# Attention and expert routing on one core: the value products of a tile shared by two heads, written alternately

## The chip, the cores and the metric

One core of a Trainium2 chip runs the whole program in one launch. The metric is device time in microseconds (us). The five engines are TensorE (PE, with its weight loads as PEld), VectorE (DVE), ScalarE (ACT), GpSimd (POOL) and SyncE (SP, which issues most DMAs).

## The reference

Eight batches of eight heads attend over 576 positions of 64 numbers. Each row of scores keeps its 32 largest, and the softmax of those weighs the values. The result, 4608 rows of 512, goes through a layer of eight experts.

```python
scores = scale * np.matmul(q, k.transpose(0, 1, 3, 2))
kth = np.partition(scores, -top_k, axis=-1)[..., -top_k:-top_k + 1]
scores = np.where(scores >= kth, scores, -1000000000.0)
attn = np.exp(scores - np.max(scores, axis=-1, keepdims=True))
attn = attn / (np.sum(attn, axis=-1, keepdims=True) + 1e-09)
return np.matmul(attn, v).astype(np.float32)
```

## The kernel before, in words

The attention (`attention`) works on 32 pairs of heads. The 576 rows of a head are four tiles of 128 and one of 64, so a pair has nine tiles: tiles 0 to 3 are the first head's, 5 to 8 the second's, and tile 4 is shared, with the last 64 rows of the first head on partitions 0 to 63 and those of the second on 64 to 127.

For each tile, `tile_ops` (L203) sets down a chain over four engines. PE computes the scores into the PSUM tile `s` (L216, one of three buffers). DVE finds the 24 largest by six partial maxima (L219) and five steps on their results (L222 to L226). ACT takes a sign (L231). PE moves the ones found out of the way (L234 with `off`), DVE finds the next eight (L237, L238), PE moves them back (L234 with `back`), and ACT writes a mask `r` (L241), which frees `s`. `soft` (L268) then computes the scores again, transposed and masked, in PSUM (L279, L284, L285). ACT takes the exponential into `F`, or into `E` for tile 4 (L289), and POOL splits `F` into two 16-bit parts `ehm` and `elm` (L292, L295). `tail` does the same for the last 64 keys, in `E4`, and in `E4r` for tile 4.

`values` (L346) multiplies the exponentials by the values. For each of the eight tiles of one head alone, `dot` sets down part 0, twelve 16-bit matmuls over four blocks of keys, and part 1, one 32-bit matmul with `E4`. Tile 4 isn't split: each of its two heads has four 32-bit matmuls with `E` as part 0 and one with `E4r` as part 1. Their weights are 64 columns wide, and the heads write to partitions 0 to 63 and 64 to 127 of one PSUM tile. All of these are L363. Then DVE adds a constant to the sums and inverts them (L343, L377), and ACT scales the rows (L345).

```python
p=None; cnt=0
for j in range(2 if g==1 else 4):
    need=[P["vready"]]+([P["ev"][4],P["e4ready"]] if g==1 else [P["ev"][j if g==0 else 5+j],P["e4op"]])
    sp=(4 if g==1 else j if g==0 else 5+j) in SPLIT
    for part in range(2):
        p=at(t0+O["vd"]*cnt,lambda j=j,part=part,dot=dot: dot(j,part),[p]+need,take="pt" if j==0 and part==0 else None,e="P",d=.224 if part else .36 if sp else .9); cnt+=1
```

The order in which each engine's instructions stand is not that of the loops. `at` hands each step to a planner (`Plan`) with a priority (a due time `t` from the table `O`), what it must follow, the engine, and a cost `d` in microseconds. `run` plays the steps through by these costs and emits each engine's instructions in the order that results. On the chip every engine then runs its instructions in that order. So a cost given to a step changes the order of all engines, while the step takes what it takes.

After attention, `logits` (L396 to L420) multiplies the rows by the gate, and the expert layer (`moe`) follows with a planner of its own.

Of the kernel before, what the change touches and what calls it, by code (L numbers as in the profile page):

```python
# [20 lines left out]
class Plan:  # L21
# [10 lines left out]
    def at(self, t, f, pre=(), take=None, free=(), e=None, d=0.0, late=0.0, order=()):  # L32

        pre, order = ([p for p in l or () if p is not None] for l in (pre, order))
        op = dict(t=t, f=f, n=len(pre) + len(order), next=[], pre=pre, order=order, take=take, left=0, free=[], e=e, d=d, late=late)
        for p in pre + order: p["next"].append(op)
        for taker in free or (): self.frees(op, taker)
        self.ops.append(op)
        return op
# [60 lines left out]
def attention(tc, q,k,v,w_gate,x_out,L,acc,cuts, pairs):  # L100
# [3 lines left out]
    with ExitStack() as ctx:  # L104
# [6 lines left out]
        V,G,A,T=nc.vector,nc.gpsimd,nc.scalar,nc.tensor  # L111
# [32 lines left out]
        at=loom.at  # L144
# [196 lines left out]
        def norm(av,n_,dst):  # L341
            r=wk.tile([128,4,1],F32,tag="rs",name="rs",bufs=4)
            V.tensor_scalar(r[:,:n_],av[:,:,64:65],VS*1e-9,None,op0=ALU.add)  # L343
            return r
        def scale(av,r,j,dst): A.activation(dst[:,j,:],av[:,j,0:64],AF.Copy,scale=r[:,j,:])  # L345
        def values(P):  # L346

            n=P["n"]; hp=P["hp"]; last=[]
            for g in (0,1,2):
                t0=(n*9+8)*PER+O["v%d"%g]  # L350
                D={}; n_=1 if g==1 else 4
                def begin(D=D,n_=n_):
                    pv=ps_t.tile([128,512],F32,tag="pt",name="pv"); D["av"]=pv[:,:n_*65].rearrange("p (j d) -> p j d",d=65)
                def dot(j,part,D=D,g=g,begin=begin):
                    if j==0 and part==0: begin()
                    av=D["av"]; vt,vh,vl=P["vt"],P["vh"],P["vl"]
                    h=0 if g==0 else 1
                    if g!=1: e_=P["e"][j if h==0 else 5+j]; out=av[:,j,:]; cs=lambda c: slice(c*128,c*128+128); last=P["e4"][:,j*128:j*128+128]
                    else: h=j; e_=P["e"][4]; out=av[h*64:h*64+64,0,:]; cs=lambda c: slice(c*128+h*64,c*128+h*64+64); last=P["e4r"]
                    if type(e_) is tuple: seq=[(e_[x][:,cs(c)],v_[:,h,c,:]) for c in range(4) for (x,v_) in ((0,vh),(0,vl),(1,vh))]  # L360
                    else: seq=[(e_[:,cs(c)],vt[:,h*5+c,:]) for c in range(4)]
                    seq.append((last,vt[:,h*5+4,:])); N=len(seq)
                    for m_ in (range(N-1) if part==0 else (N-1,)): T.matmul(out,seq[m_][0],seq[m_][1],start=(m_==0),stop=(m_==N-1))  # L363
                def dst(g=g):
                    xb,xr=P["x"]
                    return xr[:,hp:hp+1,:] if g==1 else xb[:,:,(2*hp+(0 if g==0 else 1))*64:(2*hp+(0 if g==0 else 1))*64+64]
                p=None; cnt=0
                for j in range(2 if g==1 else 4):
                    need=[P["vready"]]+([P["ev"][4],P["e4ready"]] if g==1 else [P["ev"][j if g==0 else 5+j],P["e4op"]])
                    sp=(4 if g==1 else j if g==0 else 5+j) in SPLIT  # L370
                    for part in range(2):
                        p=at(t0+O["vd"]*cnt,lambda j=j,part=part,dot=dot: dot(j,part),[p]+need,take="pt" if j==0 and part==0 else None,e="P",d=.224 if part else .36 if sp else .9); cnt+=1
                        if j==0 and part==0: tp=p
                for i in ((0,1,2,3),(4,),(5,6,7,8))[g]: loom.frees(p,P["teh"][i])
                loom.frees(p,P["te4r" if g==1 else "te4"])
                def sums(D=D,n_=n_): D["r"]=norm(D["av"],n_,None)
                def inv(D=D,n_=n_): V.reciprocal(D["r"][:,:n_],D["r"][:,:n_])  # L377
                p=at(t0+O["vd"]*cnt+O["vn"],sums,[p],e="V",d=.07); p=at(t0+O["vd"]*cnt+O["vn"]+.05,inv,[p],e="V",d=.09)
                for j in range(n_): p=at(t0+O["vd"]*cnt+O["vs"],lambda D=D,j=j,dst=dst: scale(D["av"],D["r"],j,dst()),[p],free=[tp] if j==n_-1 else None,e="A",d=.198)
                last.append(p)  # L380
            P["done"]=at(p["t"]+.001,lambda: None,last+[P["clear"]])
# [41 lines left out]
        for n in range(len(pairs)):  # L423
            prep(n); P=Ps[n]; b=P["b"]
            P.update(st=None,tr={},mx={},rel={},q2={},ev={},teh={},soft={},x=[None,None])
            first=P["hp"]==0
            def begin(P=P,n=n,first=first):
                P["st"]=wk.tile([128,9,33],F32,tag="st",name="st",bufs=3)
                P["x"]=(wk.tile([128,4,512],F32,tag="xb",name="xb",bufs=2),wk.tile([128,4,64],F32,tag="xr",name="xr",bufs=2)) if first else Ps[n-1]["x"]
            pre=[Ps[n-3]["done"]] if n>2 else []  # L430
            if n: pre.append(Ps[n-1]["begin"])
            if first and b>1: pre.append(batch[b-2])
            P["begin"]=at(n*9*PER+O["S"]-0.01,begin,pre)
            for i in range(9): tile_ops(P,i)
            for i in range(9): soft(P,i)
            clear(P)
            tail(P)
            values(P)
            if P["hp"]==2: logits(P,0)
            if P["hp"]==3:  # L440
                P["done"]=at(P["done"]["t"]+.001,lambda: None,[P["done"],Ps[n-1]["fin"]])
                logits(P,1); P["done"]=P["fin"]; batch[b]=at((n*9+8)*PER+O["lg"]+O["lgd"]*5,lambda P=P: store(P),[P["fin"]],e="D",d=2.0,late=4.0)
# [592 lines left out]
```

## Time and profile before

| | us |
|---|---|
| median of 3 runs | 1423.63 (1420.06 to 1423.87) |
| profiled execution, its own time | 1422.76 |
| its span | 1421.1 |
| PE, DVE, ACT, POOL busy | 1278.1, 1172.7, 866.8, 857.9 |
| first and last value product (L363) begins | 58.8, 941.9 |

Attention fills the first 945 us, the expert layer the rest. A matmul's busy time runs from its start until its result is written, and matmuls overlap: the one behind starts long before. So for PE's pace one reads the starts in the timeline, not the durations or the busy share.

### The profile page before, as it was taken

To read this page: it belongs to the slowest core of one execution; us is meant where nothing else is said; L and a number is where in the kernel's file an instruction comes from. 1 tells how busy PE (TensorE), PEld (TensorE's weight loads), DVE (VectorE), ACT (ScalarE), POOL (GpSimd) and SP (SyncE) were. 2 spreads that over 40 slices of the span, in tenths; PEclk is the share of its full clock that TensorE was granted. 3 is DMA by queue.
4 is the path that set the end of the run, shared out by engine and by line. 5 is a ranking of instruction groups with operands and counts; after the bars stand their busy time and mean duration, and the time that the engine had idled before them with its cause. 6 is when DMAs were issued, how large, how long until landed. Compare 5 with 4: busy or idle time off the path is not lost. (4 is left out here: it accounts for less than half of the span.)

```text
span 1421.1 us, 40893 instructions
## 1 busy us (share of the span) xinstructions
PE 1278.1 (90%) x14734; PEld 901.2 (63%) x14735; DVE 1172.7 (83%) x5815; ACT 866.8 (61%) x1906; POOL 857.9 (60%) x1285
## 2 busy tenths in 40 slices
PE   2889999999999999999999899966999999998995
PEld 1666776766777766776777677653665665664662
DVE  5899999899999999999999999948997886884520
ACT  2677777777787777778777777734432442442320
POOL 5787898789789879888878878631212212211201
PEclk8899999999999999999999999987999999999998
DMA  5344445544344454354445443214445645556301
GB/s 124 86 91 80 105 95 95 94 92 95 85 121 84 85 119 88 80 117 93 85 109 96 93 99 66 39 37 153 167 142 150 180 147 139 155 193 163 83 19 36
DMA packets 293380, 148.42 MB, mean 104 GB/s; under 512 B 250672, under 2 KB 275248, under 8 KB 292144
## 3 DMA queue, kind: packets, MB, share of 16 engines
q1 hardware_dynamic: 287280, 126.84, 38.6%
q0 software_dynamic: 5888, 18.88, 4.4%
q8 instruction: 117, 1.92, 0.6%
q14 instruction: 95, 0.78, 0.2%
HBM read 71.34 MB, written 18.87 MB: 63 GB/s over the span
## 5 line engine op out<-in xcount | busy, mean ns | idle before, releaser
L219 DVE MAX8 cd<-s 128x8 f32<-128x96 f32 x1728 | 373.0, 252 | 34.9 <-PE s L216 30.2
L295 POOL TENSOR_TENSOR elm<-F,ehm 128x512 f16<-128x512 f32 x256 | 294.5, 1157 | 7.9
L241 ACT ACTIVATE r<-s,st 128x576 bf16<-128x576 f32 x288 | 213.2, 740 | 106.5 <-PE s L234 70.7
L231 ACT ACTIVATE w<-s,st 128x576 uint16<-128x576 f32 x288 | 213.5, 741 | 79.9 <-DVE st L227 76.9
L238 DVE MAX8 st<-s 128x8 f32<-128x584 f32 x288 | 220.7, 766 | 7.6 <-PE s L234 2.9
L216 PE MATMUL s<-K,Q 128*128 128x512 f16 (+3 forms) x1280 | 192.8, 291 | 27.7 <-DMA Q<-nq 20.1
L928 PE MATMUL ph<-xT,w1h 128*128 128x288 f16 x1024 | 190.8, 287 | 0.0
L285 PE MATMUL pt<-Q,K 66*128 66x128 f16 (+1 forms) x1280 | 179.0, 216 | 0.0
L284 PE MATMUL pt<-Q,K 128*128 128x128 f16 (+1 forms) x1280 | 178.2, 215 | 0.0
L292 POOL TENSOR_SCALAR ehm<-F 128x512 f16<-128x512 f32 x256 | 156.8, 618 | 32.4 <-ACT F L289 30.0
L886 POOL DMA_INDIRECT xg<-x,idx x40 | 45.0, 1125 | 213.9 <-DVE idx L836 114.0
L216 PEld LDWEIGHTS <-Q 128*128 128x128 f16 (+1 forms) x1280 | 104.8, 103 | 108.2 <-DMA Q<-nq 19.8
L234 PE MATMUL s<-w,off 128*128 128x512 f16 x576 | 132.7, 288 | 38.5 <-DVE s L237 30.3
L289 ACT ACTIVATE F<-pt 128x512 f32<-128x512 f32 x256 | 150.7, 596 | 14.7 <-PE pt L285 8.2
L363 PE MATMUL pv<-vt,E 128*64 128x65 f32 (+1 forms) x1024 | 146.7, 257 | 0.3 <-DVE L L414 0.3
L928 PE MATMUL ph<-xT,w1l 128*128 128x288 f16 x512 | 146.9, 287 | 0.0
L971 POOL DMA_INDIRECT out_dram<-ob,idx x40 | 42.7, 1068 | 167.3 <-ACT ob L962 120.5
L234 PE MATMUL s<-w,back 128*128 128x512 f16 x576 | 118.8, 288 | 20.6 <-DVE st L238 18.3
L284 PEld LDWEIGHTS <-K 128*128 128x128 f16 x1280 | 117.2, 99 | 18.2 <-issue 5.3
L363 PEld LDWEIGHTS <-ehm 128*128 128x128 f16 x2048 | 115.9, 101 | 9.8
L363 PEld LDWEIGHTS pv<-vt,E 128*64 128x64 f32 (+1 forms) x1024 | 113.1, 164 | 13.5 <-issue 3.1
L363 PE MATMUL pv<-vl,ehm 128*128 128x65 f16 x1024 | 120.8, 192 | 0.0
(279 smaller groups left out, 3198.1 us busy)
## 6 DMA issues: line engine op xcount, KB each, us to landing
wr<-in_moe_w_dram SPq DMA_DIRECT2D x32, 1024.0 KB, 8.4
kn<-in_k_dram SPq DMA_DIRECT2D x64, 128.0 KB, 2.6
qn<-in_q_dram SPq DMA_DIRECT2D x64, 128.0 KB, 2.3
vn<-in_v_dram SPq DMA_DIRECT2D x64, 128.0 KB, 2.3
x<-xb SPq DMA_DIRECT2D x8, 1024.0 KB, 4.3
Q<-nq SPq DMA_TRANSPOSE x160, 3.2
kn<-in_k_dram SPq DMA_DIRECT2D x64, 16.0 KB, 2.3
qn<-in_q_dram SPq DMA_DIRECT2D x64, 16.0 KB, 2.2
```

Source lines behind the costliest of these rows:

```text
L216: T.matmul(s_ps[rows,a:b_],P[Q][:,qc],P[K][:,h*576+a:h*576+b_],start=(Q=="Q1"),stop=(Q=="Q2"))
L219: V.max(D["cd"][:,c*8:c*8+8],D["s"][:,576*c//NCH:576*(c+1)//NCH])
L231: A.activation(D["w"],D["s"][:,:576],AF.Sign,bias=P["st"][:,i,32:33],scale=(1+2.0**-21),accum_out=acc[:,col])
L234: T.matmul(D["s"][:,a:b_],by,w[:,a:b_],start=False,stop=True,skip_group_check=True)
L238: def next8(): V.max(P["st"][:,i,24:32],D["s"][:,:584])
L241: A.activation(r,D["s"][:,:576],AF.Relu,bias=P["st"][:,i,31:32],scale=-1.0)
L284: T.matmul(o,K2[:,kb:kb+128],Q1[:,qc],start=False,stop=False,skip_group_check=True)
L285: T.matmul(o,K3[0:66,kb:kb+128],Q2[0:66,qc],start=False,stop=(c==3 and h==sub[-1][0]),skip_group_check=True)
L292: G.tensor_scalar(D["eh"],D["E"],1.0,0.0,op0=ALU.mult,op1=ALU.add)
L295: G.tensor_tensor(el,D["E"],D["eh"],op=ALU.subtract); P["e"][i]=(D["eh"],el)
L363: for m_ in (range(N-1) if part==0 else (N-1,)): T.matmul(out,seq[m_][0],seq[m_][1],start=(m_==0),stop=(m_==N-1))
L928: P.matmul(B["ph"][:,:288],a[:,c,fs],xT[:,b+c,cs],start=(i==0),stop=(i==11))
```

## The change

The two heads' products of tile 4 become one step instead of two. Within it each matmul of the first head is followed by the same one of the second, so that the two halves of the PSUM tile are written in turn. Part 0 holds the eight matmuls with `E`, part 1 the two with `E4r`. The costs handed to the planner change too: for tile 4 .5 and .14 for both heads together, where each head had .9 and .224; for the other tiles part 0 goes from .36 to .38, and part 1 from .224 to .14. The table `O` of due times is as it was.

```diff
-                    h=0 if g==0 else 1
-                    if g!=1: e_=P["e"][j if h==0 else 5+j]; out=av[:,j,:]; cs=lambda c: slice(c*128,c*128+128); last=P["e4"][:,j*128:j*128+128]
-                    else: h=j; e_=P["e"][4]; out=av[h*64:h*64+64,0,:]; cs=lambda c: slice(c*128+h*64,c*128+h*64+64); last=P["e4r"]
...
-                    for m_ in (range(N-1) if part==0 else (N-1,)): T.matmul(out,seq[m_][0],seq[m_][1],start=(m_==0),stop=(m_==N-1))
+                    for h in ((0,1) if g==1 else (0 if g==0 else 1,)):
...
+                        runs.append((o_,seq+[(last,vt[:,h*5+4,:])]))
+                    N=len(runs[0][1])
+                    for m_ in (range(N-1) if part==0 else (N-1,)):
+                        for o_,seq in runs: T.matmul(o_,seq[m_][0],seq[m_][1],start=(m_==0),stop=(m_==N-1),skip_group_check=(g==1))
...
-                for j in range(2 if g==1 else 4):
+                for j in range(1 if g==1 else 4):
...
-                        p=at(t0+O["vd"]*cnt,lambda j=j,part=part,dot=dot: dot(j,part),[p]+need,take="pt" if j==0 and part==0 else None,e="P",d=.224 if part else .36 if sp else .9); cnt+=1
+                        p=at(t0+O["vd"]*cnt,lambda j=j,part=part,dot=dot: dot(j,part),[p]+need,take="pt" if j==0 and part==0 else None,e="P",d=((.14 if part else .5) if g==1 else .14 if part else .38 if sp else .56)); cnt+=1
```

Because costs change, the orders of PE, DVE, ACT, POOL and SP all differ from the first pair's products on. They hold the same instructions. In the changed file lines behind this place are two further on (L363 is L365).

On PE, behind the scores and products of the sixteenth pair, the shared tile's products stood so before. A row of the 32-bit products is one matmul of the program, which the trace shows as two; x4 are the four key blocks of one head; `E` is tile 4's exponentials:

```order
L216 MATMUL s<-K_10483,Q_10556 128x64
L234 LDWEIGHTS back
L234 MATMUL s<-w,back 128x512
L234 LDWEIGHTS back
L234 MATMUL s<-w,back 128x64
L363 MATMUL pv<-vt_187,E 64x65 x4
L363 MATMUL pv<-vt_187,E4r 64x65
L234 LDWEIGHTS off
L234 MATMUL s<-w,off 128x512
L234 LDWEIGHTS off
L234 MATMUL s<-w,off 128x64
L363 MATMUL pv<-vt_187,E 64x65 x4
```

The second head's E4r product stands thirteen rows further on, behind one more tile's scores and a move back. With the change the same pair has:

```order
L234 LDWEIGHTS back
L234 MATMUL s<-w,back 128x512
L234 LDWEIGHTS back
L234 MATMUL s<-w,back 128x64
L234 LDWEIGHTS off
L234 MATMUL s<-w,off 128x512
L234 LDWEIGHTS off
L234 MATMUL s<-w,off 128x64
L365 MATMUL pv<-vt_187,E 64x65 x8
L365 MATMUL pv<-vt_187,E4r 64x65 x2
L216 LDWEIGHTS Q_10625
L216 MATMUL s<-K_10382,Q_10625 128x512
```

The three visits to 64-wide products have become one, and it stands ahead of the next tile's scores (L216) instead of around them.

On DVE, in the same pair, the sums of the shared tile (L343 of 128x1) stood among the partial maxima of a tile whose scores PE had computed between the heads:

```order
L225 MATCH_REPLACE cd_11298<-st,cd_11298 128x48
L226 MAX st<-cd_11298 128x8
L219 MAX cd<-s 128x8 x3
L343 TENSOR_SCALAR rs<-pv 128x1
L219 MAX cd<-s 128x8
L377 RECIPROCAL rs<-rs 128x1
```

With the change they stand behind the search for the next eight of an earlier tile:

```order
L225 MATCH_REPLACE cd_11243<-st,cd_11243 128x48
L238 MAX st<-s 128x8
L343 TENSOR_SCALAR rs<-pv 128x1
L226 MAX st<-cd_11243 128x8
L379 RECIPROCAL rs<-rs 128x1
L227 SCALAR_TENSOR_TENSOR st<-s,st 128x1
L219 MAX cd<-s 128x8 x3
```

The sums have moved ahead of the next tile's maxima, as their products on PE have moved ahead of that tile's scores.

## Rows read from the trace of the kernel before

**Rows 1.** The page: busy time of each engine; one group of DVE.

```profile
PE 1278.1 (90%) x14734; PEld 901.2 (63%) x14735; DVE 1172.7 (83%) x5815; ACT 866.8 (61%) x1906; POOL 857.9 (60%) x1285
...
L238 DVE MAX8 st<-s 128x8 f32<-128x584 f32 x288 | 220.7, 766 | 7.6 <-PE s L234 2.9
```

**Rows 2.** Busy time by stretch: attention's second half, and the expert layer.

```profile
core 0: us, PE busy (x) PEld busy (x) DVE busy (x) ACT busy (x) POOL busy (x), PEclk, DMA share, GB/s
450.00:850.00 400.00, 372.93 (x5099) 281.53 (x5097) 374.51 (x2157) 309.75 (x718) 336.17 (x520) 1.00 0.46 95
...
945.00:1421.00 476.00, 428.02 (x3205) 261.31 (x3204) 320.06 (x917) 163.58 (x280) 87.73 (x80) 0.94 0.43 129
```

**Rows 3.** Waits of DVE, 50 to 900 us (total, times, longest).

```profile
DVE cd L219 <- PE s L216: 14.5, 39, 1.4
DVE s L237 <- ACT w L231: 6.6, 27, 0.4
```

**Rows 4.** Busy time in one pair: its products, its shared tile, the rest.

```profile
486.00:493.90 7.90, 7.76 (x138) 6.43 (x136) 7.49 (x47) 4.92 (x14) 7.15 (x10) 1.00 0.70 89
493.90:498.80 4.90, 4.53 (x46) 3.21 (x45) 4.69 (x26) 3.72 (x11) 3.69 (x8) 1.00 0.75 109
498.80:514.40 15.60, 14.03 (x177) 10.34 (x177) 14.58 (x85) 12.60 (x27) 10.70 (x19) 1.00 0.51 152
```

**Rows 5.** Timeline of PE, shared tile (start, us, engine line op, shape, count).

```profile
495.00 0.41 PE L234 MATMUL s<-w,back 128*128 128x512 f16 x2
495.34 0.68 PE L363 MATMUL pv<-vt,E 128*64 128x65 f32 x8
495.85 0.28 PE L363 MATMUL pv<-vt,E4r 128*64 128x65 f32 x2
496.50 0.41 PE L234 MATMUL s<-w,off 128*128 128x512 f16 x2 [0.37 <-DVE s L237]
496.84 0.68 PE L363 MATMUL pv<-vt,E 128*64 128x65 f32 x8
497.45 0.66 PE L216 MATMUL s<-K,Q 128*128 128x512 f16 x4
...
498.29 0.33 PE L363 MATMUL pv<-vt,E4r 128*64 128x65 f32 x2
498.45 0.35 PE L408 MATMUL lg<-wgr,xT 128*64 128x8 f32 x4
```

**Rows 6.** Timeline of PE, one tile of a single head.

```profile
488.54 0.42 PE L234 MATMUL s<-w,back 128*128 128x512 f16 x2
488.79 0.19 PE L363 MATMUL pv<-vh,ehm 128*128 128x65 f16 x1
...
489.16 0.41 PE L363 MATMUL pv<-vt,E 128*128 128x65 f32 x2
489.41 0.19 PE L363 MATMUL pv<-vh,ehm 128*128 128x65 f16 x1
```

**Rows 7.** Timeline of PE, shared tile of the last pair.

```profile
940.93 0.74 PE L363 MATMUL pv<-vt,E 128*64 128x65 f32 x10 [0.26 <-DVE L L414]
941.45 0.22 PE L363 MATMUL pv<-vt,E4r 128*64 128x65 f32 x1
941.50 0.22 PE L363 MATMUL pv<-vt,E 128*64 128x65 f32 x1
941.51 0.22 PE L363 MATMUL pv<-vt,E4r 128*64 128x65 f32 x1
941.56 0.45 PE L363 MATMUL pv<-vt,E 128*64 128x65 f32 x5
941.85 0.28 PE L363 MATMUL pv<-vt,E4r 128*64 128x65 f32 x2
941.97 0.35 PE L408 MATMUL lg<-wgr,xT 128*64 128x8 f32 x4
```

More of the change, by code (lines that the diff above doesn't have):

```diff
@@ L355, in dot @@
                     if j==0 and part==0: begin()
-                    av=D["av"]; vt,vh,vl=P["vt"],P["vh"],P["vl"]
-                    h=0 if g==0 else 1
-                    if g!=1: e_=P["e"][j if h==0 else 5+j]; out=av[:,j,:]; cs=lambda c: slice(c*128,c*128+128); last=P["e4"][:,j*128:j*128+128]
-                    else: h=j; e_=P["e"][4]; out=av[h*64:h*64+64,0,:]; cs=lambda c: slice(c*128+h*64,c*128+h*64+64); last=P["e4r"]
-                    if type(e_) is tuple: seq=[(e_[x][:,cs(c)],v_[:,h,c,:]) for c in range(4) for (x,v_) in ((0,vh),(0,vl),(1,vh))]
-                    else: seq=[(e_[:,cs(c)],vt[:,h*5+c,:]) for c in range(4)]
-                    seq.append((last,vt[:,h*5+4,:])); N=len(seq)
-                    for m_ in (range(N-1) if part==0 else (N-1,)): T.matmul(out,seq[m_][0],seq[m_][1],start=(m_==0),stop=(m_==N-1))
+                    av=D["av"]; vt,vh,vl=P["vt"],P["vh"],P["vl"]; runs=[]
+                    for h in ((0,1) if g==1 else (0 if g==0 else 1,)):
+                        if g!=1: e_=P["e"][j if h==0 else 5+j]; o_=av[:,j,:]; cs=lambda c: slice(c*128,c*128+128); last=P["e4"][:,j*128:j*128+128]
+                        else: e_=P["e"][4]; o_=av[h*64:h*64+64,0,:]; cs=lambda c,h=h: slice(c*128+h*64,c*128+h*64+64); last=P["e4r"]
+                        if type(e_) is tuple: seq=[(e_[x][:,cs(c)],v_[:,h,c,:]) for c in range(4) for (x,v_) in ((0,vh),(0,vl),(1,vh))]
+                        else: seq=[(e_[:,cs(c)],vt[:,h*5+c,:]) for c in range(4)]
+                        runs.append((o_,seq+[(last,vt[:,h*5+4,:])]))
+                    N=len(runs[0][1])
+                    for m_ in (range(N-1) if part==0 else (N-1,)):
+                        for o_,seq in runs: T.matmul(o_,seq[m_][0],seq[m_][1],start=(m_==0),stop=(m_==N-1),skip_group_check=(g==1))
                 def dst(g=g):
```

## The prediction

> **What bounds the kernel now.** I read the page first, then the busy time by stretch, then who waited for whom, and last PE's timeline at the shared tile. The page shows PE busiest [rows 1], but a matmul counts as busy until its result is written, so this overstates PE. By stretch, DVE is busy 374.51 of 400 us in the second half of attention and PE 372.93, at a granted clock of 1.00 [rows 2]: two engines are close to full, and neither waits long for the other. DVE's longest wait on another engine is for the scores, 14.5 us in 39 waits between 50 and 900 us; the next is for ACT's sign, 6.6 us [rows 3]. The rest of DVE's idle time, some 25 of the 400 us, is largely gaps between its own dependent steps. So the pace of attention is DVE's, with PE a little behind. Within a pair PE is tightest in the stretch of single-head products, 7.76 busy of 7.90 us, and has some air afterwards, 4.53 of 4.90 and 14.03 of 15.60 [rows 4]. The expert layer [rows 2] is planned apart and isn't touched.
>
> **What the shared tile costs PE.** The starts give the pace. Eight records of one head take 0.51 us, from 495.34 to 495.85, so 0.06 to 0.065 each; two of E4r take about 0.12. Two heads make 2 x (0.51 + 0.12) = 1.26 us a pair [rows 5]. Going to 64-wide weights costs something too: from the move back at 495.00 to the first product is 0.34 us, where a full-width product follows the same move after 0.25 [rows 5, 6], so 0.09 to enter; and the eight records at 496.84 take 0.61 up to the next full-width matmul instead of 0.51, so 0.10 to leave [rows 5]. A visit costs 0.19. Counted over the whole order the change has 37 visits fewer: 37 x 0.19 = 7 us of PE.
>
> **Do two halves run at once in 32 bits?** This decides the main saving, and one place shows it. In the last pair the two heads stand directly behind each other, and there an E record of the second head starts at 941.50 and an E4r record of the first at 941.51; the 20 records end, by the start of the next line, at 941.97, so they took 1.04 us instead of 1.26 [rows 7]. Where a neighbour of the other half is in sight, PE runs both. Alternated throughout, I take 10 steps of 0.06 = 0.60 us a pair, so 0.66 saved, 32 x 0.66 = 21 us of PE, and with the visits 28 us, some 0.85 to 0.9 a pair. The Trainium skill ("TensorE: Matmul & The Clock Gate", part 3, The mechanism) says that weight loads overlap with running matmuls only where the row groups differ, and that matmuls start in strict order. Both heads use all 128 rows, so by that rule the alternation would save nothing but the visits. Rows 7 speak against it here: E4r of the first head starts behind an E of the second, which stands later in the program. The rule's own outcome is rival 3.
>
> **What of it lies on the path.** PE time only counts where DVE waits for PE. In the stretch of the shared tile DVE is idle 4.90 - 4.69 = 0.21 us [rows 4]. Over 32 pairs that is 6.7 us, the most that can come back there if nothing else moves, and zero is the least if those gaps are DVE's own. I take half, 3.4 us. In the last pair nothing runs beside PE, and 1.04 us becomes about 0.6 [rows 7]: 0.4 us more. Together -3.8 us.
>
> **What the planner is now told.** The costs change for all products, and an order made with wrong costs puts work where PE isn't ready. Part 0 of a single-head tile takes 0.37 us, from 488.79 to 489.16; the table says .38 instead of .36, both right. Part 1 takes 0.25, from 489.16 to 489.41 [rows 6]; the table said .224 and now says .14. Eight a pair: PE used to be 8 x 0.026 = 0.2 us later than planned at the end of the products, and now 8 x 0.11 = 0.9, so about 0.67 more a pair. The shared tile was planned at 2.25 and took 1.26 and two or three visits, about 1.7, so it gave 0.5 back; now it is planned at .64 and should take 0.60 + 0.19. So the order used to be a little pessimistic over a pair and becomes optimistic by about 1 us, in the stretch in which PE has 0.14 us to spare [rows 4]. The lateness is used up in the 15.6 us that follow, where PE has 1.57 idle [rows 4]. DVE can lose between nothing (it has other tiles' maxima to do, since three score buffers are in turn) and all of the 0.67, 32 x 0.67 = 21 us. Now DVE feels PE's scores in 39 of some 270 tiles, one in seven [rows 3]; in the densest stretch it will be more, and I take a fifth: +4.3 us.
>
> **The rest.** DVE holds the same 5,682 rows in both orders, and ACT, POOL and SP the same instructions in another order. DVE's sums of the shared tile move ahead of the next maxima, but so do their products on PE; in the order shown, the search for the next eight stands between (0.77 us [rows 1]), so the products of 0.8 us are nearly covered. I cost these at nothing; were the cover gone, it would be 0.1 us a pair, 3 us, which the range holds. POOL's splits and SP's transposes keep their sequence around the products and have idle time there, 15.60 - 10.70 in POOL's case [rows 4].
>
> **Sum.** Against the profiled execution's 1422.76: -3.8 + 4.3 = +0.5, 1423.3 us. That execution was 0.9 below the median of the runs, and the answer is a median, so I forecast 1424.2 us, no change. A measurement of this kernel can tell about 0.3%, 4.3 us, so no change means 1419.4 to 1427.9.
>
> **Rivals.**
> 1. *Slower: the planned lateness reaches DVE.* Place: the eight part-1 products, where the order now expects 0.14 and gets 0.25. DVE's maxima (L219) stand waiting for scores that PE issues late, and later waits follow since ACT's sign and PE's moves of that tile start late as well. It decides from the point where a share x of the 21 us outweighs the gain by 4.3, 21x - 3.8 > 4.3, x over 0.38. At two thirds it is 14.3 - 3.8, so 1434; in full 1441. For it: PE's 0.14 us of air in this stretch, and a 0.67 us swing in eight places. Against it: DVE's named waits are short now, though PE is nearly full. Chance 0.33.
> 2. *Faster: PE is the pace after all.* PE and DVE are busy to within 2 us of each other [rows 2], and many of DVE's gaps could be PE's lateness at one remove. If half of the 28 us saved comes through, 14, less the 4.3 that the order costs and with the 0.4 of the tail, it is 10 less: 1414. For it: 372.93 of 400, and the saving falls right behind the tightest stretch. Against it: the shared tile lies where PE already waits for others, 0.37 us for DVE between the two heads [rows 5]. Chance 0.27.
> 3. *The halves don't overlap.* Only the visits are saved, 0.2 us a pair of PE; the shared tile takes 1.26 + 0.19 where .64 is planned, so 0.66 more lateness a pair. At a fifth that is +4.2, and the gain shrinks from 3.8 to about 1: 1431. Rows 7 speak against it. Chance 0.03.
>
> **How the numbers follow.** Forecast 0.37 (1424.2, its own range 1419 to 1428); rival 1 0.33 and rival 3 0.03, slower, 0.36; rival 2 0.27, faster. The range from 1409 to 1441 takes in rival 2 a little beyond its middle and rival 1 to its full price; what it leaves out is PE's saving coming through almost whole, and waits that multiply, about 0.2 together.
>
> **What would show it.** The shared tile's E records starting in pairs a few ns apart, 16 in about 0.5 us, and fewer entries to 64-wide weights: the saving is real. DVE's wait for L216 grown by a few us in the products' stretch: the order's cost. If it stays at 14.5 and DVE's busy share rises over 94%, rival 2; if it grows by 10 or more, rival 1. If the E records still step by 0.06, rival 3. A change in the expert layer's 476 us would mean that I have overlooked something.

## The result, and the profile after

The changed kernel takes 1433.44 us (median of 5 runs, 1430.22 to 1435.60), the kernel before 1423.63: a ratio of 1.0073, with a 95% interval of 1.005 to 1.0096. It is slower by 9.8 us: inside the range, near the price of the first rival (1434) and not at the forecast of no change.

The page of the changed kernel, busy time of each engine:

```profile
PE 1267.5 (89%) x14734; PEld 886.9 (62%) x14735; DVE 1175.9 (82%) x5815; ACT 863.0 (60%) x1906; POOL 860.5 (60%) x1285
```

PE is busy 10.6 us less than in [rows 1], with as many instructions, and the span is 10.8 us longer. Busy time by stretch, columns as in [rows 2]:

```profile
50.00:450.00 400.00, 360.67 (x5012) 269.92 (x5012) 369.92 (x2118) 303.00 (x707) 331.66 (x514) 0.99 0.46 94
450.00:850.00 400.00, 361.51 (x5003) 270.47 (x5003) 372.61 (x2121) 302.55 (x708) 332.40 (x513) 1.00 0.46 94
```

In the second stretch PE fell from 372.93 to 361.51 us and DVE got through 2,121 instructions instead of 2,157 [rows 2], 1.7% fewer, with a granted clock of 1.00 in both. Attention is slower on DVE, while PE has more air. Attention's last product begins at 949.8 instead of 941.9, so some 8 of the 10.8 us of span are there; the expert layer's part is 481.9 us behind the last product against 478.9, with a longer stretch at the lower clock at its start. Over all the kernels traced here this part runs from 477.2 to 481.9 us, and in the fastest kernel of all (experiment 6) it is 481.7, so its 3 us can't be put down to the change.

The shared tile itself does what it should. PE's timeline, sixteenth pair:

```profile
497.95 0.19 PE L234 MATMUL s<-w,off 128*128 128x64 f16 x1 [0.32 <-DVE s L237]
498.07 0.69 PE L365 MATMUL pv<-vt,E 128*64 128x65 f32 x16
498.59 0.29 PE L365 MATMUL pv<-vt,E4r 128*64 128x65 f32 x4
498.81 0.61 PE L216 MATMUL s<-K,Q 128*128 128x512 f16 x2
```

From the first E record to the first E4r record it is 0.52 us for sixteen, where it was 0.51 for eight [rows 5]. In the trace the two heads' records mostly start 5 to 7 ns apart. From the first product to the scores behind it is 0.74 us, one visit. Not every pair comes down to one: over all of attention the trace shows 163 entries to 64-wide weights, of any product, against 200 before, so the 37 fewer that the prediction counted.

What DVE waits for, 50 to 900 us (total, times, longest), against [rows 3]:

```profile
DVE cd L219 <- PE s L216: 14.3, 40, 1.3
DVE s L237 <- PE s L234: 8.3, 33, 0.7
DVE s L237 <- ACT w L231: 2.3, 9, 0.3
DVE st L238 <- PE s L234: 1.8, 10, 0.3
DVE rs L343 <- PE pv L365: 1.4, 6, 0.3
```

and, in the kernel before, the three that [rows 3] leaves out:

```profile
DVE rs L343 <- PE pv L363: 0.8, 4, 0.2
DVE st L238 <- PE s L234: 0.8, 4, 0.3
DVE s L237 <- PE s L234: 0.7, 3, 0.3
```

The wait for scores is as it was, 14.3 against 14.5. New is the fill's (L237) for PE's first half of the move, 8.3 us, where it had 0.7. In part it only takes the place of another: the fill's wait for ACT's sign fell from 6.6 to 2.3, so all that the fill waits for went from 7.3 to 10.6. The five lines together went from 23.4 to 28.1, 4.7 us more, while attention got some 8 us longer; the rest is in no wait that is named here. A fill and that half of the move write the same `s`, and whichever the planner emits second waits for the other; the planner doesn't know of this. In the new order 111 fills of 288 come second, before 85.

### The profile page after: what moved, and what is told of

It reads as the page before. It is cut to its first block, busy times and chain, and to the rows that moved or that the text cites. A ratio compares the mean times of both kernels' runs of the same rounds, so it can differ in the third digit from the quotient of the medians.

```text
span 1431.9 us, 40896 instructions
## 1 busy us (share of the span) xinstructions
PE 1267.5 (89%) x14734; PEld 886.9 (62%) x14735; DVE 1175.9 (82%) x5815; ACT 863.0 (60%) x1906; POOL 860.5 (60%) x1285
## 5 line engine op out<-in xcount | busy, mean ns | idle before, releaser
L219 DVE MAX8 cd<-s 128x8 f32<-128x96 f32 x1728 | 372.8, 251 | 33.9 <-PE s L216 29.8
L216 PE MATMUL s<-K,Q 128*128 128x512 f16 (+3 forms) x1280 | 192.5, 291 | 32.1 <-DMA Q<-nq 20.2
L285 PE MATMUL pt<-Q,K 66*128 66x128 f16 (+1 forms) x1280 | 182.0, 215 | 0.6 <-DMA Q<-nq 0.6
L284 PE MATMUL pt<-Q,K 128*128 128x128 f16 (+1 forms) x1280 | 181.5, 215 | 0.0
L234 PE MATMUL s<-w,off 128*128 128x512 f16 x576 | 137.0, 288 | 49.6 <-DVE s L237 37.5
L216 PEld LDWEIGHTS <-Q 128*128 128x128 f16 (+1 forms) x1280 | 105.6, 102 | 117.5 <-issue 21.9
L234 PE MATMUL s<-w,back 128*128 128x512 f16 x576 | 118.5, 287 | 29.4 <-DVE st L238 14.5
L365 PE MATMUL pv<-vt,E 128*64 128x65 f32 (+1 forms) x1024 | 125.5, 257 | 0.3 <-DVE L L416 0.3
L365 PEld LDWEIGHTS <-ehm 128*128 128x128 f16 x2048 | 118.3, 102 | 7.3
L365 PE MATMUL pv<-vl,ehm 128*128 128x65 f16 x1024 | 120.7, 192 | 0.0
L365 PE MATMUL pv<-vh,ehm 128*128 128x65 f16 x1024 | 120.7, 195 | 0.0
```

The lines of the kernel that those rows point to most:

```text
L216: T.matmul(s_ps[rows,a:b_],P[Q][:,qc],P[K][:,h*576+a:h*576+b_],start=(Q=="Q1"),stop=(Q=="Q2"))
L219: V.max(D["cd"][:,c*8:c*8+8],D["s"][:,576*c//NCH:576*(c+1)//NCH])
L234: T.matmul(D["s"][:,a:b_],by,w[:,a:b_],start=False,stop=True,skip_group_check=True)
L284: T.matmul(o,K2[:,kb:kb+128],Q1[:,qc],start=False,stop=False,skip_group_check=True)
L285: T.matmul(o,K3[0:66,kb:kb+128],Q2[0:66,qc],start=False,stop=(c==3 and h==sub[-1][0]),skip_group_check=True)
L365: for o_,seq in runs: T.matmul(o_,seq[m_][0],seq[m_][1],start=(m_==0),stop=(m_==N-1),skip_group_check=(g==1))
```

## Experiments

**Theory A:** the new order costs time, because it is made with costs that PE can't keep, and the alternation itself gains (A1: it is the low cost of part 1). **Rival B:** the alternation costs on the chip. **Rival D:** any new plan under the old due times loses. Before's median beside these runs was 1422.9 to 1423.4. Of long lines the diffs show only the end that changes.

**1. The new order with the heads behind each other.**

```diff
-                    for m_ in (range(N-1) if part==0 else (N-1,)):
-                        for o_,seq in runs: T.matmul(...)
+                    for o_,seq in runs:
+                        for m_ in (range(N-1) if part==0 else (N-1,)): T.matmul(...)
```

> The changed kernel's order of all engines, but on PE the shared tile's eight E matmuls stand head behind head instead of in turn (and so do the two E4r). Theory A (the new order costs, the alternation itself gains): slower than the changed kernel by what the alternation is worth, 2 to 8 us, so 1435 to 1441. Rival B (the alternation itself costs on the chip, by switching between halves): faster than the changed kernel, 1430 or less. If alternation is worth nothing: 1433.

Measured 1442.93 us, ratio 1.0127 (1.0109 to 1.0145). So in this order the alternation gains 9.5 us, and the order without it, with the two heads in one step but behind each other, costs 19.5. Even behind each other the heads overlap a little on PE, sixteenth pair:

```profile
501.87 0.79 PE L365 MATMUL pv<-vt,E 128*64 128x65 f32 x13
502.45 0.27 PE L365 MATMUL pv<-vt,E4r 128*64 128x65 f32 x1
502.50 0.22 PE L365 MATMUL pv<-vt,E 128*64 128x65 f32 x1
502.56 0.22 PE L365 MATMUL pv<-vt,E4r 128*64 128x65 f32 x1
502.56 0.28 PE L365 MATMUL pv<-vt,E 128*64 128x65 f32 x2
502.68 0.28 PE L365 MATMUL pv<-vt,E4r 128*64 128x65 f32 x2
```

The last record starts about 0.87 us after the first, against some 0.59 when alternated: 0.3 us a pair. DVE's instructions stand in the same order in both runs, so I set the starts of the same 1,728 partial maxima (L219) side by side: this run falls behind by 0.29 us in nearly every pair, and by 1.1 to 1.5 us more at each of three short stretches at the lower clock that the other doesn't have. The 0.29 alone makes about 9 us over 32 pairs, so in this order nearly all of PE's time at the shared tile comes out on DVE. Rival B falls.

**2. The old order with the alternation.**

```diff
                     if j==0 and part==0: begin()
+                    if g==1 and j==1: return
...
+                    for m_ in (range(N-1) if part==0 else (N-1,)):
+                        for o_,seq in runs: T.matmul(...)
```

The planner still sees two steps with the old costs; the first issues both heads.

> The order and costs of the kernel before; only both heads' products of the shared tile are issued in turn at the first head's places, and nothing at the second's. Theory A: the gain without its price, 2 to 8 us faster than before, so 1416 to 1422; PE's E records start in pairs a few ns apart. Rival B: slower than before, over 1426.

Measured 1425.18 us, ratio 1.0012 (1.0002 to 1.0023). Neither expectation is met: it gains nothing. Its fastest execution, 1420.57, is level with the fastest of the kernel before beside it, 1420.75, so the lower clock told of below doesn't hide a gain. The profiled execution is the slowest of its twelve, 1428.86. Side by side with the kernel before, in the same order, it is 0.07 to 0.65 us ahead up to 382 us, mostly 0.1 to 0.3, and doesn't pull away. Then it loses 3.1 us twice and otherwise stays level. Both losses are stretches at half clock. Busy time by stretch in the kernel before (columns as in [rows 2]):

```profile
380.00:388.00 8.00, 7.14 (x74) 5.02 (x74) 7.65 (x47) 6.07 (x17) 4.79 (x11) 1.00 0.54 109
388.00:396.00 8.00, 7.31 (x105) 5.89 (x103) 7.39 (x41) 6.54 (x14) 5.38 (x9) 1.00 0.27 66
...
500.00:504.00 4.00, 3.10 (x35) 2.41 (x34) 3.86 (x26) 2.83 (x8) 0.92 (x4) 1.00 0.29 80
504.00:512.00 8.00, 7.71 (x111) 5.55 (x109) 7.39 (x41) 6.66 (x13) 7.41 (x10) 1.00 0.52 165
```

and with the alternation in the same order:

```profile
380.00:388.00 8.00, 6.48 (x67) 4.28 (x64) 7.65 (x49) 6.11 (x16) 4.72 (x10) 1.00 0.57 118
388.00:396.00 8.00, 7.60 (x56) 6.14 (x56) 4.59 (x23) 3.94 (x8) 3.83 (x7) 0.57 0.28 76
...
500.00:504.00 4.00, 2.64 (x20) 1.53 (x18) 3.80 (x25) 3.37 (x10) 1.16 (x1) 1.00 0.77 146
504.00:512.00 8.00, 7.53 (x55) 6.08 (x55) 4.59 (x24) 3.88 (x8) 3.75 (x7) 0.57 0.25 70
```

Ahead of the first PE is busy 6.48 of 8 us instead of 7.14, ahead of the second 2.64 of 4 instead of 3.10. Then the granted clock is 0.57 on average, the half level of 1.2 GHz for most of the stretch, and DVE gets through 23 or 24 instructions where it did 41. Each time the lower clock came right behind a stretch in which PE had been busy less; that this is why isn't shown, since no run forces it. The executions of this kernel go from 1420.57 (mean clock 0.981) to 1428.86 (0.970).

**3. The cost changes alone, and alone the other one.** The kernel before, its shared tile as it was:

```diff
-d=.224 if part else .36 if sp else .9)
+d=(.224 if part else .9) if g==1 else .14 if part else .38)
```

> The kernel before with the new planned costs of the single-head products alone (.38 and .14 for .36 and .224), the shared tile as before. Theory A1 (the slowdown comes from the part-1 cost that is too low, 0.14 against 0.25 in the trace): slower than before by 8 to 16 us, 1432 to 1440. Rival C (the low cost is harmless, and the new shared step moves the order): within 4 us of before, 1420 to 1428.

Measured 1441.16 us, ratio 1.012 (1.0106 to 1.0135): just above A1's range. The new costs of the single-head products cost 17.8 us without the new step. The .38 for .36 came with the .14, and this run doesn't part the two; A1 takes it to be the .14 for a product that takes 0.25. Its waits, 50 to 900 us:

```profile
DVE cd L219 <- PE s L216: 19.6, 60, 0.4
DVE s L237 <- PE s L234: 6.9, 22, 0.4
DVE st L238 <- PE s L234: 6.1, 24, 0.4
DVE rs L343 <- PE pv L363: 2.5, 14, 0.2
```

All four of DVE's waits for PE are longer: in the kernel before they were 14.5 [rows 3], 0.7, 0.8 and 0.8 us.

The changed kernel with the old single-head costs:

```diff
-.14 if part else .38 if sp else .56))
+.224 if part else .36))
```

> The changed kernel with the old planned costs of the single-head products (.36 and .224) and the new ones of the shared tile (.5 and .14). Theory A1 (the low part-1 cost is what hurts): faster than before by 1 to 8 us, 1416 to 1423. Rival D (any re-planning with the old due times loses, whichever cost is changed): still slower than before, 1428 to 1436. By the fills that wait for PE (125 in this order, 111 in the changed kernel's, 85 before) it would be the slowest, 1436 or more.

Measured 1431.39 us, ratio 1.0062 (1.0048 to 1.0077): rival D's number, not A1's. The guess from the fills fails as well: 125 of them wait for PE here, and it is no slower than the kernel with 111. At this point A and D stood level.

**4. Measured costs, high costs, and a harmless new plan.** The changed kernel with what the traces measure:

```diff
-d=((.14 if part else .5) if g==1 else .14 if part else .38 if sp else .56)
+d=((.14 if part else .69) if g==1 else .25 if part else .37)
```

> The changed kernel, planned with what the traces measure: single-head products .37 and .25, the shared tile .69 (0.50 and 0.19 for the visit) and .14. Theory A (orders made with too low costs lose, since PE comes late): 1420 to 1426, as before or a little less. Rival D (with the due times as they were, any new plan loses, right or wrong in its costs): 1428 to 1442, as the three new plans so far (1431, 1433, 1441).

Measured 1419.32 us, ratio 0.9977 (0.9967 to 0.9986). The same edit, the same due times, other costs: 14 us faster than the changed kernel, and 3.6 faster than the kernel before. Rival D falls in its strict form. Nor is it the distance from the old order that costs: of DVE's instructions in attention, counted place by place, 37% stand where they stood before, against 52% in the changed kernel.

With the old sum of costs for the shared step:

```diff
+d=((.45 if part else 1.8) if g==1 else .224 if part else .36)
```

> The changed kernel with the old planned costs throughout: .36 and .224 for single heads, and for the shared tile's step 1.8 and .45, the sum of what its two heads had. The plan believes about as much PE time as the plan before. Theory A: PE is ahead of the plan again, so 1418 to 1426. Rival D: another order, so 1428 or more.

Measured 1452.82 us, ratio 1.0216 (1.0199 to 1.0233). A miss for A as I had put it: being ahead of the plan is no help. With the shared tile as a single step that is planned at 2.25 us and takes 0.8, the kernel is 30 us slower than before, though two steps planned at 1.12 didn't hurt the kernel before.

The kernel before with .37 for .36:

> The kernel before, not alternated, with one planned cost moved by 0.01 us, part 0 of single heads from .36 to .37, which is what the trace measures. Nothing else changes but the order that comes out. Theory A: within 4 us of before, 1420 to 1428. Rival D: slower by 5 to 15 us, 1428 to 1438, with no wrong cost in it.

Measured 1423.98 us, ratio 1.0009 (0.9999 to 1.0018): this new order costs nothing. It is a weak test of D, since 89% of DVE's instructions in attention stay at their place; the order of 1419.32 above and that of 1426.02 below (58%) test it better.

**5. The fill put ahead of the move.**

```diff
-p=at(t0+O["wm"],lambda: move(off,0),[p],e="P",d=0.216)
+p=at(t0+O["wm"],lambda: move(off,0),[p],e="P",d=0.216,order=[f_])
```

> The changed kernel with one more rule for the planner: the first half of the move (L234, off) goes behind the start of its tile's fill (L237), so that no fill waits for PE's move (111 do in the changed kernel, 85 before). If the fill's waits on PE, 8 us more than before between 50 and 900 us, are what the new order loses: 1422 to 1428. If they are only where a lateness from elsewhere shows: 1430 to 1437. If the move then waits for DVE instead and the chain gets longer: over 1438.

Measured 1462.71 us, ratio 1.0288 (1.0271 to 1.0306), the third case. Its waits:

```profile
DVE cd L219 <- PE s L216: 31.0, 63, 0.8
DVE st L238 <- PE s L234: 10.8, 44, 1.2
```

The fill's wait is gone and the scores' has doubled. But the rule makes another order altogether (18% of DVE's instructions in attention stand where the changed kernel has them), so the run doesn't tell whether the fill's 8.3 us were a cost of their own; it shows that this rule doesn't get them back.

**6. Which of the two costs, and the alternation's share.** Single heads as measured, shared tile at the changed kernel's .5:

```diff
+d=((.14 if part else .5) if g==1 else .25 if part else .37)
```

> The changed kernel with the measured costs of the single-head products (.37 and .25) and its own low one of the shared tile (.5 and .14, the 0.19 of the visit left out). Theory A, if the single-head cost is what did the harm: 1417 to 1426. If the shared tile's missing 0.19 is enough to lose: 1428 to 1433, like the run with .36 and .224 beside it (1431).

Measured 1418.47 us, ratio 0.9967 (0.9956 to 0.9979), the fastest of all. Busy time and waits:

```profile
450.00:850.00 400.00, 368.27 (x5102) 277.03 (x5100) 376.70 (x2157) 308.76 (x721) 335.72 (x522) 1.00 0.46 97
```

```profile
DVE cd L219 <- PE s L216: 10.9, 33, 0.8
DVE st L238 <- PE s L234: 3.0, 16, 0.2
DVE s L237 <- PE s L234: 2.9, 17, 0.2
DVE s L237 <- ACT w L231: 1.6, 8, 0.2
```

The fill's wait for PE is back from 8.3 to 2.9 us, that for scores down from 14.3 to 10.9. DVE's order is nearly that of the run with measured costs (97% at the same place), so the two good runs are one order rather than two.

The other half:

```diff
+d=((.14 if part else .69) if g==1 else .14 if part else .38)
```

> The other half: the changed kernel's single-head costs (.38 and .14) with the shared tile at .69 and .14. Theory A, if the single-head cost did the harm: 1430 to 1440. If the shared tile's cost did it: 1417 to 1426. If both fall here, near 1420, only the two errors together lose; if both lose, plans near the measured costs scatter by 10 us and 1419 was a lucky one.

Measured 1453.49 us, ratio 1.0216 (1.0194 to 1.0237). Of the two costs it is the single-head one whose correction takes the loss away. The size is a miss for A, above its 1440: with the shared tile planned rightly the loss is larger than with it planned wrongly, 1453 against 1433, so it isn't a sum of errors.

The order of the run with measured costs, heads behind each other (edit as in 1):

> The order of the run with measured costs (1419), with the shared tile's heads behind each other on PE, 0.5 us more per pair. What the alternation is worth in an order planned for it: 5 to 12 us by the pair of runs on the changed kernel's order (1433 and 1443), so 1424 to 1431; if PE's time at this place is off the path as in the old order, 1419 to 1421.

Measured 1422.30 us, ratio 0.9995 (0.9985 to 1.0005): the alternation is worth about 3 us in an order planned for it, between the two cases. Side by side the serial run falls behind by about 0.1 us a pair, a third of what it did in the changed kernel's order.

The kernel before with measured costs throughout:

```diff
-d=.224 if part else .36 if sp else .9)
+d=(.14 if part else .7) if g==1 else .25 if part else .37)
```

> The kernel before, not alternated, planned with measured costs: .37 and .25 for single heads, .70 and .14 for each head of the shared tile. If the 1419 came from right costs alone: 1417 to 1422. If the alternation has a share: 1422 to 1427, as before. By the scatter of plans: anything up to 1435.

Measured 1426.02 us, ratio 1.0026 (1.0013 to 1.0039). Right costs alone, without the alternation, give nothing; with it, in another order, 1419.3 and 1418.5.

All plans by their single-head costs (the trace measures .37 and .25), without the runs that change only what stands inside the shared tile's step and without experiment 5:

| part 0, part 1 | shared step planned | alternated | us |
|---|---|---|---|
| .37, .25 | .5 + .14 | yes | 1418.5 |
| .37, .25 | .69 + .14 | yes | 1419.3 |
| .37, .25 | 2 x (.7 + .14) | no | 1426.0 |
| .37, .224 | 2 x (.9 + .224) | no | 1424.0 |
| .36, .224 (before) | 2 x (.9 + .224) | no | 1423.6 |
| .36, .224 | .5 + .14 | yes | 1431.4 |
| .36, .224 | 1.8 + .45 | yes | 1452.8 |
| .38, .14 (the change) | .5 + .14 | yes | 1433.4 |
| .38, .14 | 2 x (.9 + .224) | no | 1441.2 |
| .38, .14 | .69 + .14 | yes | 1453.5 |

The three with .14 are some 10 us or more slower than before. Of the three with .25, two of them nearly one order, none is more than 3 us slower.

## Why the prediction was right or wrong

*The forecast of no change was wrong; rival 1 named the cause, and its price came out by luck.* The step that failed is the term for "what the planner is now told". I had bounded it between 0 and 21 us and taken a fifth, 4.3, from the one tile in seven in which DVE waits for scores. The new order without the alternation costs 19.5 us (experiment 1) and the new single-head costs without the new step 17.8 (experiment 3), nearly the upper end. Counting waits that exist in the old order said nothing of those that a wrong order makes. Rival 1's 1434 was 14.3 us lost less 3.8 gained; the runs show 19.5 and 9.5, two misses that make up for each other.

*The gain was mis-sized too.* I had taken 3.8 us from DVE's idle time in that stretch of the old order. In the old order the alternation is some 0.3 us ahead side by side and gives nothing in the median (1425.18 against 1423.40); that reading was right in kind, and half of 6.7 was too much. In the new order it gives 9.5, because there PE's time at the shared tile comes out on DVE nearly in full. The sum added a gain read in the old order to a price paid in the new one, as if neither hung on the other. That 19.5 - 9.5 = 10.0 lies near the measured 9.8 is no check: experiment 1 stands in both numbers, and what is left is the changed kernel against the kernel before once more.

*The mechanism on PE was right.* The halves overlap in 32 bits (sixteen E records in the time of eight), and the entries to 64-wide weights fell by the 37 counted. Rival 3 falls with it. So does, for these two column halves, the rule of the Trainium skill that the prediction set beside it ("TensorE: Matmul & The Clock Gate", part 3, The mechanism), that weight loads overlap with running matmuls only where the row groups differ: both heads use all 128 rows, and their records mostly start 5 to 7 ns apart.

*The place named for rival 1 was wrong.* I expected longer waits for L216 in the products' stretch; over attention they stayed at 14.3 us. The named wait that grew is the fill's for PE's move, and more than half of that was taken from its wait for ACT. Whether the lateness comes from there or only shows there, experiment 5 leaves open: it came out in its third case, in an order of its own.

*The expert layer* was to show what I had overlooked. It is 3 us longer behind the last product, but so is that of the fastest kernel, and the clock at its start differs from trace to trace.

*Rival 2* describes the two runs with measured single-head costs and the alternation, not the change as made: they are 3.6 and 4.8 us faster than before, and about 3 of that is PE's saving at the shared tile (experiment 6).

What stays open is the size for each wrong plan. A .224 planned with the alternated step loses 8 us and the same with two old steps nothing; a wrong .14 costs 20 us more with the right shared cost than with the low one. Within these runs, right single-head costs and the alternation together win, but in what is nearly one order, so a lucky order isn't ruled out; the path from one wrong number to its microseconds isn't shown.

## What to carry to other kernels

Where a planner sets the order, a cost handed to it is part of the kernel: read each from the starts in the trace, for the very shape (a 64-column product's pace isn't that of a 128-column one), before judging the edit that came with it. Test an edit in a fixed order first, then the new order without the edit; here that split a loss of 10 us into a gain of 9.5 and a cost of 19.5. And time saved on an engine gains nothing where that engine isn't the pace, as in experiment 2.

## What the runs showed of the hardware

The lower clock came where I had not looked. In the slowest execution of experiment 2, PE was busy 6.48 of 8 us and 2.64 of 4, some 0.7 and 0.5 us less than in the kernel before, and right behind each of the two stood a stretch with a granted clock of 0.57 that cost 3.1 us; that the one brings the other isn't shown. PE also doesn't keep the order of its instructions across the two column halves. In experiment 1, where all E records stand ahead of all E4r records, the first head's E4r records start at 502.45 and 502.56, ahead of the last E records of the second head (502.50 to 502.62). So with its parts together even the serial form takes about 0.9 us, and not 1.26.
